# Second dense layer: plain products for the first 512 tokens, seven-product blocks of 448 for the rest

## The chip, the cores and the metric

One Trainium2 chip; the program uses one of its cores. The time of a run is the device time in microseconds (us), from one launch. Three runs of the kernel before gave 692.82, 694.65 and 697.71 us; their median is 694.65 us. TensorE is called PE, VectorE DVE, ScalarE ACT, GpSimd POOL and SyncE SP, as in the profile.

## What is computed

Three stages follow one another: a Nystrom attention over 4 batches of 576 tokens (8 heads of 64), a mixture of 8 experts with one expert for each token, and a dense layer. All of it is in float32. The dense layer, which the change touches, is this, with x the 2304 x 512 output of the experts:

```
h = x @ w_in                   # 512 -> 2048
r = np.maximum(h, 0.0)
g = s * (r * r) + b
out = g @ w_out                # 2048 -> 512
```

## The kernel before, in words

Float32 products are made on PE from operands of type fp32r: each operand is split into a high and a low part (h = cast(x), l = x - h), and `mm3` (L969) issues three matmuls, high x high, high x low and low x high, into one PSUM bank. A matmul has a 128 x 128 stationary block and up to 512 columns of the moving operand, and here the columns are tokens. All matmuls of the experts and of the dense layer have the line L972.

The work order is not written out by hand. Every operation is handed to a planner (`Plan`) with an engine, an expected duration, what it reads and writes, a priority and operations that it must follow (`after`). `Plan.run` lists all of them in time; each engine then executes its list strictly in that order, and semaphores hold an instruction until its inputs are there. Copies and casts (`copy`) go to ACT or DVE, additions and subtractions (`minus`) to DVE or POOL, as the planner chooses.

**The dense layer before.** Tokens are taken in three groups G of 768, each of two blocks of NT = 384 (`layer2`, L1163). For each of 8 units j, the hidden rows 128j to 128j+127 and 1024+128j to 1024+128j+127 are made: two row blocks, two halves of the 512 inputs, two token blocks. Such a 2 x 2 x 2 product takes seven block products instead of eight (Strassen-Winograd), so a unit has 7 x 6 = 42 matmuls in the first product (`prod`, called l3 here). The price is additions: four of the tokens, in `tokens` (tiles tq), four of the weights in each unit, in `weights` (tiles sx), and those of the products, in `take` and `plus` (tiles xx), done by ACT and DVE. Then `square` makes g from each of four results: relu on ACT (L1202), times s and itself on DVE (L1203), high part on ACT (L1206), low part on DVE (L1208). The second product (l4) has 4 output blocks dc x 2 token blocks th x 6 = 48 matmuls in a unit. For th = 0 the sum stays in four PSUM banks (`acc2`); for th = 1 there is one bank (`accr`), which DVE adds to a stored sum (L1250, tiles sums) before the next th = 1 product may start.

**What else lies in the first group.** In G = 0 the unit's weights are split by ACT, DVE and POOL from w_in (tiles w32i) into sh, so and sx (`weights`, L1107) and from w_out (w32o) into oh and ol (`outer`, L1144), and the parts are stored in DRAM by ACT's queue (sw_d, so_d). Groups 1 and 2 only load them back, by SP's queue (tiles rh, ro, rx and rp, rq). The weights arrive as 8-byte numbers, and `convert` (L1037) turns them into float32 by three DVE operations (L1042, L1049, L1051), two on ACT and one on POOL (L1054) for each of 32 pieces. These conversions start during the experts and run on into G = 0. `tokens` splits each group's seven operands into th and a low half that overwrites its source; it is called for G = 0 after the last batch's first products (`t_at`), and for G + 1 after unit 6 of G (`ahead`). Token blocks that wait are kept in DRAM (y_d).

Of the kernel before, what the change touches and what calls it, by code (L numbers as in the profile page):

```python
# [314 lines left out]
def d_dma(nbytes):  # L315
    return nbytes / RATE


TUNE = {"ahead": (6,), "t_at": lambda st: [st[B - 1]["l1half"]], "w_at": lambda st: [st[B - 1]["l1first"]], "blk": "AADD", "pre": 2, "bias": {"DVE": 0.3, "ACT": 0.0},
        "flex": {"w2l": "P", "al": "P"}, "fill": 45.0, "slack": 0.05, "duty": 0.45, "first": 12,  # L320
# [19 lines left out]
def moe_kernel(ctx, tc, qT, kT, va, vb, emb, tau, w1, w2, win, wout, s_in, b_in, outT):  # L340
# [13 lines left out]
    big = ps.tile([128, 8, 512], F32, name="big")  # L354
# [64 lines left out]
    b_row = [fixed(row_d) for _ in range(B)]  # L419
    y_d = dr.tile([2 * NG, 2, 128, 2, NT], F32, name="y_d")  # L420
    sw_d, so_d = dr.tile([8, 128, 28, 128], F32, name="sw_d"), dr.tile([8, 2, 128, 2, 512], F32, name="so_d")
# [541 lines left out]
    def low(b):  # L963

        if b.rest is None:
            b.rest = at(b, b.shape, F32R)
        return b.rest
# [105 lines left out]
    ops2 = {}  # L1073
# [4 lines left out]
    def tokens(G, first, then):  # L1078

        pr = 30000 + 1000 * G - 500  # L1080
        back = []
        for i in (2 * G, 2 * G + 1):
            if not G:
                back.append(y[i])
                continue
# [12 lines left out]
        minus(n, v(b12), v(b22), v(b12), "ta", r=[b22], w=[b12], prio=pr + 1, after=first)  # L1098
        minus(n, v(t4), v(b21), v(t2), "ta", r=[b21, t2], w=[t4], prio=pr + 1)
        ops2[G] = {}  # L1100
        for i, (p, b) in enumerate(((1, b11), (2, b21), (5, t1), (6, t2), (7, b12), (4, t4), (3, b22))):
            h = S_([128, 2, NT], F32R, nm="th")
            copy(n, v(h), v(b), "yh", r2=True, r=[b], w=[h], prio=pr + 2 + i, after=first if i < 2 else then)
            minus(n, lambda b=b: low(b), v(b), lambda h=h: h.t.bitcast(F32), "yl", r=[h], w=[b], prio=pr + 2 + i)
            ops2[G][p] = (h, b)

    def weights(G, j, pr, after):  # L1107

        a, d, js = w32i[j // 2], w32i[j // 2 + 4], 128 * (j % 2)
        q = lambda b, c, n=2: lambda: b.t[:, c:c + n, js:js + 128]  # L1110
        if G:
            sx, sh, so = (S_([128, n, 128], F32R, nm=nm) for n, nm in ((8, "rx"), (14, "rh"), (6, "ro")))
            for b, o, n in ((sh, 0, 14), (so, 14, 6), (sx, 20, 8)):
                dma(512 * 128 * n, lambda b=b, o=o, n=n: nc.sync.dma_start(b.t.bitcast(F32), sw_d[j, :, o:o + n, :]), r=[(c_sw, (j, o))], w=[b],
                    prio=pr, kind="lds", after=after)
            return choose(sx, sh, so, lambda: sx.t, 0)
# [12 lines left out]
        for b, o, n, v in ((sh, 0, 14, lambda: sh.t), (so, 14, 6, lambda: so.t), (sx, 20, 8, lambda: low(sx))):  # L1129
            store(512 * 128 * n, lambda o=o, n=n, v=v: nc.scalar.dma_start(sw_d[j, :, o:o + n, :], v().bitcast(F32)), r=[b], w=[(c_sw, (j, o))],  # L1130
                  prio=pr + 4, kind="sts")
        return choose(sx, sh, so, lambda: low(sx), 1)

    def choose(sx, sh, so, rest, parts):
# [9 lines left out]
    def outer(G, j, pr, first):  # L1144
# [16 lines left out]
        return oh, ol  # L1161

    def layer2(G):  # L1163
        mm = (NT + 32) / 2400.0
# [6 lines left out]
        def unit(j, last, early):  # L1171
            pu = pr + 10 * j
            left = weights(G, j, pu - 10, [ops2["firsts"][-2 if G else -1]] if last else TUNE["w_at"](st))
            bank = {k: Q("hp2") for k in "abc"}
# [25 lines left out]

            def square(i, src, b):
                A("ACT", d_actp(NT), lambda: nc.scalar.activation(out=rr[i].t, in_=src(), func=AF.Relu), r=[b], w=[rr[i]], prio=pu, kind="rr")  # L1202
                A("DVE", d_dve(NT), lambda: nc.vector.scalar_tensor_tensor(  # L1203
                    out=rr[i].t, in0=src(), scalar=sbc[:, 0:1], in1=rr[i].t, op0=ALU.mult, op1=ALU.mult), r=[b, (c_sb, 0)],
                  w=[rr[i]], prio=pu, kind="q")
                A("ACT", d_act(NT), lambda: nc.scalar.activation(  # L1206
                    out=gh[i].t, in_=rr[i].t, func=AF.Identity, bias=bbc[:, 0:1]), r=[rr[i], (c_sb, 1)], w=[gh[i]], prio=pu, kind="gh")
                A("DVE", d_dve(NT), lambda: nc.vector.scalar_tensor_tensor(  # L1208
                    out=low(rr[i]), in0=rr[i].t, scalar=bbc[:, 0:1], in1=gh[i].t.bitcast(F32), op0=ALU.add, op1=ALU.subtract),
                  r=[gh[i], (c_sb, 1)], w=[rr[i]], prio=pu, kind="gl")  # L1210
            first = prod(1, "a", [(b, -1) for b in rr + gh], [last] if last else [st[B - 1]["l1last"]])
# [4 lines left out]
            square(0, view(x11), x11)  # L1216
            full = prod(5, "c", after=[two_])
# [4 lines left out]
            plus(x22, "a")  # L1222
            square(3, view(x22), x22)
            prod(4, "a")
            square(2, pv("a"), bank["a"])
            prod(3, "c")
            plus(x12, "c")
            square(1, view(x12), x12)
            if G + 1 < NG and j == TUNE["ahead"][0]:
# [4 lines left out]
            for dc in range(4):  # L1234
                for th in range(2):
# [19 lines left out]
                    if j == 7:  # L1255
                        ob = sums[dc]
                        if not th:
                            ob = S_([128, NT], nm="ob")
                            copy(NT, view(ob), lambda ac=ac: ac.t[:, 0:NT], "ob", ps=True, r=[ac], w=[ob], prio=pu + 15)
                        t0 = 2 * NT * G + NT * th  # L1260
                        dma(128 * 4 * NT, lambda dc=dc, ob=ob, t0=t0: nc.sync.dma_start(
# [22 lines left out]
    def second_layer(gates):  # L1284
        convert_all(gates)
        for i in range(2, 2 * NG):
            for c, b in enumerate(y[i]):
                b.keep = False
                store(256 * 4 * NT, lambda i=i, c=c, b=b: nc.scalar.dma_start(y_d[i, c], b.t), r=[b], w=[(c_yd, (i, c))],
                      prio=4000 + 500 * i, kind="spy")  # L1290
        tokens(0, TUNE["t_at"](st), TUNE["t_at"](st))
        for G in range(NG):
            layer2(G)
# [97 lines left out]
```

## Time and profile before

| | |
|---|---|
| runs, us | 692.82, 694.65, 697.71 (median 694.65) |
| profiled execution, us | 691.78 |
| its span from the first to the last instruction, us | 689.9 |
| mean granted TensorE clock, share of 2.4 GHz | 0.979 |
| PE busy | 645.2 us (94%), 5066 matmuls |
| DVE, ACT, POOL busy | 487.7, 304.9, 229.0 us (71%, 44%, 33%) |
| DMA moved | 132.98 MB |

An engine's busy time counts the time in which it has at least one instruction; a matmul's own duration is longer than the distance to the next, since matmuls overlap. Stages are read from the times of the program's tiles: the experts end and the dense layer begins at 271.6 us, and PE's last matmul starts at 682.5 us.

### The profile page before, as it was taken

The page shows a single profiled execution, that of the slowest core. Times are in us where ns is not written, and L with a number is a line of the kernel's source. Part 1 is how long each engine was busy: PE and PEld are TensorE (multiplying, and loading weights), DVE is VectorE, ACT ScalarE, POOL GpSimd, SP SyncE. Part 2 cuts the span into 40 slices and gives each one's busy share as a digit, 9 for nine tenths or more (in the row PEclk, how much of TensorE's full clock was granted, in tenths as well). Part 3 has the DMA queues.
Part 4 walks back from the last instruction along what each step waited for, and adds up shares of the span by engine and source line. Part 5 has one row for each costly group of instructions (what it writes and reads, how often), then busy time and mean ns, then how long its engine had stood idle before and what let it go on. Part 6 is the DMA issues. An engine that isn't in the chain of part 4 may idle for free.

```text
span 689.9 us, 13153 instructions
## 1 busy us (share of the span) xinstructions
PE 645.2 (94%) x5066; PEld 601.5 (87%) x5066; DVE 487.7 (71%) x1015; ACT 304.9 (44%) x634; POOL 229.0 (33%) x197
## 2 busy tenths in 40 slices
PE   7799989999999999889879989999998999999995
PEld 5577778878998999789779878999998999999995
DVE  6976678696687789999788895645557754556551
ACT  2257345545546545555344542533335344333331
POOL 3633531523455756764356761000006200000000
PEclk9999999999999999999889999999999999999999
DMA  6619763765568382457553648844556476555102
GB/s 220 229 45 337 249 192 120 242 188 186 172 195 266 126 296 107 198 199 259 199 206 146 229 182 271 293 169 168 191 206 229 150 273 236 203 179 195 63 0 97
DMA packets 55576, 132.98 MB, mean 193 GB/s; under 512 B 5024, under 2 KB 25032, under 8 KB 55504
## 3 DMA queue, kind: packets, MB, share of 16 engines
q1 hardware_dynamic: 46208, 101.74, 43.8%
q10 hardware_dynamic: 9296, 30.30, 11.3%
q8 instruction: 42, 0.69, 0.4%
q14 instruction: 30, 0.25, 0.1%
HBM read 98.19 MB, written 33.84 MB: 191 GB/s over the span
## 4 chain that ended last, share of the span: by engine, by line
PE 72%; DVE 18%; ACT 3%; DMA 3%; issue 2%; SPq 1%; POOL 1%; DVEq 0%; ACTq 0%; POOLq 0%
PE big L972 64%; DVE rr L1208 4%; DVE rr L1203 3%; DMA vv<-in_va 2%; PE big L825 2%; PE big L945 1%; DVE xx L1198 1%; DVE y L1076 1%; PE big L644 1%; PE big L723 1%; DVE sums L1250 1%; PE big L699 1%; DMA w1s<-in_w 1%; DVE tq L1076 1%; PE big L687 1%
## 5 line engine op out<-in xcount | busy, mean ns | idle before, releaser
L1250 DVE TENSOR_TENSOR sums<-big,sums 128x384 f32<-128x384 f32 x84 | 46.6, 554 | 60.7 <-PE big L972 60.5
L972 PE MATMUL big<-gh,rp 128*128 128x384 f32 x256 | 86.4, 337 | 3.0 <-DVE sums L1250 3.0
L972 PE MATMUL big<-gh,rq 128*128 128x384 f32 x256 | 86.2, 337 | 0.0
L972 PE MATMUL big<-rr,rp 128*128 128x384 f32 x256 | 86.1, 336 | 0.0
L1208 DVE SCALAR_TENSOR_TENSOR rr<-rr,bbc,gh 128x384 fp32r<-128x384 f32 x96 | 75.2, 804 | 5.9 <-ACT gh L1206 5.9
L972 PE MATMUL big<-hh,w2h 128*128 128x288 f32 x256 | 78.3, 306 | 0.0
L1206 ACT ACTIVATE gh<-rr,bbc 128x384 fp32r<-128x384 f32 x96 | 58.5, 617 | 41.1 <-DVE rr L1203 39.8
L972 PE MATMUL big<-hl,w2h 128*128 128x288 f32 x256 | 75.7, 296 | 0.0
L1198 DVE TENSOR_TENSOR xx<-big,xx 128x384 f32<-128x384 f32 x72 | 39.7, 555 | 50.6 <-PE big L972 50.0
L972 PE MATMUL big<-hh,w2s 128*128 128x288 f32 x256 | 75.2, 294 | 0.0
L972 PE MATMUL big<-th,rh 128*128 128x384 f32 x224 | 75.0, 335 | 0.0
L508 ACT COPY xx<-big 128x384 f32<-128x384 f32 x55 | 26.0, 474 | 88.8 <-PE big L972 88.3
L1202 ACT ACTIVATE rr<-xx 128x384 f32<-128x384 f32 x72 | 37.8, 525 | 60.4 <-DVE xx L1198 60.2
L1203 DVE SCALAR_TENSOR_TENSOR rr<-xx,sbc,rr 128x384 f32<-128x384 f32 x72 | 53.3, 746 | 11.9 <-ACT rr L1202 9.5
L972 PE MATMUL big<-gh,oh 128*128 128x384 f32 x128 | 47.0, 367 | 8.9 <-DVE sums L1250 8.1
L972 PEld LDWEIGHTS big<-hh,w2h 128*128 128x128 f32 x256 | 48.0, 187 | 4.3 <-issue 3.1
L972 PEld LDWEIGHTS big<-gh,rp 128*128 128x128 f32 x256 | 48.6, 190 | 3.3 <-DVE sums L1250 3.3
L959 POOL TENSOR_TENSOR w2s<-w2s,w2h 128x1024 fp32r<-128x1024 f32 x16 | 38.3, 2413 | 32.1 <-PE big L945 18.1
L972 PEld LDWEIGHTS big<-rr,rp 128*128 128x128 f32 x256 | 48.6, 190 | 0.0
L972 PEld LDWEIGHTS big<-gh,rq 128*128 128x128 f32 x256 | 48.5, 190 | 0.0
L972 PE MATMUL big<-rr,oh 128*128 128x384 f32 x128 | 45.8, 358 | 2.7 <-DVE rr L1208 2.7
L972 PEld LDWEIGHTS big<-hl,w2h 128*128 128x128 f32 x256 | 48.1, 188 | 0.2 <-DVE hl L1000 0.2
(242 smaller groups left out, 1726.6 us busy)
## 6 DMA issues: line engine op xcount, KB each, us to landing
rh<-sw_d SPq DMA_DIRECT2D x16, 896.0 KB, 6.8
w1s<-in_w SPq DMA_DIRECT2D x16, 512.0 KB, 5.5
w2s<-in_w SPq DMA_DIRECT2D x16, 512.0 KB, 4.8
sg<-in_win SPq DMA_DIRECT2D x16, 512.0 KB, 5.1
sg<-in_wout SPq DMA_DIRECT2D x16, 512.0 KB, 3.9
rx<-sw_d SPq DMA_DIRECT2D x16, 512.0 KB, 3.9
rp<-so_d SPq DMA_DIRECT2D x16, 512.0 KB, 3.7
rq<-so_d SPq DMA_DIRECT2D x16, 512.0 KB, 4.6
```

The source lines that it names most:

```text
L508: nc.scalar.copy(out=out(), in_=in_()) if e == "ACT" else nc.vector.tensor_copy(out=out(), in_=in_())
L644: nc.tensor.matmul(xp.t[r_, 64 * g + 32 * lo:64 * g + 64], cur()[r_, g, 0, :], cur()[r_, g, lo:2, :], start=True, stop=True)
L825: nc.tensor.matmul(xp.t[:n, g, 0:264], s_[g].t[:, t0:t0 + n], m_.t[:, g, :], start=(i == 0), stop=(i == 2))
L959: two(1024, lambda e, ws=ws, wh=wh: e.tensor_tensor(out=low(ws), in0=ws.t, in1=wh.t.bitcast(F32), op=ALU.subtract), "w2l", r=[wh], w=[ws], ...
L972: nc.tensor.matmul(out, w, x, start=s, stop=e, skip_group_check=more)
L1076: return two(n, lambda e: e.tensor_tensor(out=out(), in0=a(), in1=b(), op=op), kind, **kw)
L1198: A("DVE", d_dve(NT), lambda: nc.vector.tensor_tensor(out=x.t, in0=pv(k)(), in1=x.t, op=ALU.add), r=[bank[k]], w=[x], prio=pu, kind="l6")
L1202: A("ACT", d_actp(NT), lambda: nc.scalar.activation(out=rr[i].t, in_=src(), func=AF.Relu), r=[b], w=[rr[i]], prio=pu, kind="rr")
L1203: A("DVE", d_dve(NT), lambda: nc.vector.scalar_tensor_tensor(out=rr[i].t, in0=src(), scalar=sbc[:, 0:1], in1=rr[i].t, op0=ALU.mult, op1=AL ...
L1206: A("ACT", d_act(NT), lambda: nc.scalar.activation(out=gh[i].t, in_=rr[i].t, func=AF.Identity, bias=bbc[:, 0:1]), r=[rr[i], (c_sb, 1)], w= ...
L1208: A("DVE", d_dve(NT), lambda: nc.vector.scalar_tensor_tensor(out=low(rr[i]), in0=rr[i].t, scalar=bbc[:, 0:1], in1=gh[i].t.bitcast(F32), op ...
L1250: nc.vector.tensor_tensor(out=sums[dc].t, in0=ac.t[:, 0:NT], in1=sums[dc].t, op=ALU.add)
```

## The change

The first 512 tokens become a block of their own, in which the first product is made plainly: per unit two row blocks x four pieces of the input x three = 24 matmuls of 512 columns, and 24 for the second product, with all sums kept in PSUM (`first_block`). Its weights are the plain parts ph and pl (`plain`). The other 1792 tokens are two groups of two blocks of 448 with seven products as before. Group 1 makes and stores the sums and parts of the seven products' weights, group 2 loads them; oh and ol are made and stored in the first block, and both groups load them. `ahead` goes from unit 6 to unit 3, and the first weights and tokens are released somewhat later (`w_at`, `t_at`). Buffers for ph and pl are new; lines that only rename are left out here.

```diff
-NT, NG = 384, 3
-BLOCKS = [(NT * i, NT) for i in range(2 * NG)]
+NT, NG = 448, 3
+BLOCKS = [(0, 512)] + [(512 + NT * i, NT) for i in range(4)]
...
-TUNE = {"ahead": (6,), "t_at": lambda st: [st[B - 1]["l1half"]], "w_at": lambda st: [st[B - 1]["l1first"]], "blk": "AADD", "pre": 2, "bias": {"DVE": 0.3, "ACT": 0.0},
+TUNE = {"ahead": (3,), "s_at": 2, "t_at": lambda st: [st[B - 1]["l1last"]], "w_at": lambda st: [st[B - 1]["l1half"]], "blk": "AADD", "pre": 2, "bias": {"DVE": 0.3, "ACT": 0.0},
...
+        if not G:
+            ops2[0] = []
+            for b in y[0]:
+                b.keep = False
+                h = S_([128, 2, 512], F32R, nm="th")
+                copy(1024, lambda h=h: h.t, lambda b=b: b.t, "yh", r2=True, r=[b], w=[h], prio=pr, after=first)
+                minus(1024, lambda b=b: low(b), lambda b=b: b.t, lambda h=h: h.t.bitcast(F32), "yl", r=[h], w=[b], prio=pr)
+                ops2[0].append((h, b))
+            return
...
-        if G:
+        if G == 2:
...
+    def plain(j, pr, after):
+
+        js, out = 128 * (j % 2), []
+        for a in (w32i[j // 2], w32i[j // 2 + 4]):
+            h, l = (S_([128, 4, 128], F32R, nm=nm) for nm in ("ph", "pl"))
+            src = lambda a=a: a.t[:, :, js:js + 128]
+            copy(512, lambda h=h: h.t, src, "wsh", r2=True, r=[a], w=[h], prio=pr, after=after)
+            minus(512, lambda l=l: l.t, src, lambda h=h: h.t.bitcast(F32), "wsl", r=[a, h], w=[l], prio=pr)
+            out.append((h, l))
+        return out
...
+    def first_block():
+        n = BLOCKS[0][1]
+        mm, pr = (n + 32) / 2400.0, 30000
+        acc, xs = [Q("acc2") for _ in range(4)], ops2[0]
...
+        def unit(j, last):
+            pu = pr + 10 * j
+            left = plain(j, pu - 10, last[:1] if last else TUNE["w_at"](st))
+            rr, gh = [S_([128, n], nm="rr") for _ in range(2)], [S_([128, n], F32R, nm="gh") for _ in range(2)]
+            done = []
+            for x in range(2):
+                bank, (h, l) = Q("hp2"), left[x]
+
+                def f(bank=bank, h=h, l=l):
+                    for c in range(4):
+                        xh, xl = xs[c // 2]
+                        mm3(bank.t[:, 0:n], (h.t[:, c, :], l.t[:, c, :]), (xh.t[:, c % 2, :], low(xl)[:, c % 2, :]), c == 0, c == 3)
...
+                square(n, rr[x], gh[x], lambda bank=bank: bank.t[:, 0:n], bank, pu)
...
+            if j == TUNE["ahead"][0]:
+                tokens(1, [done[0]], [done[0]])
+            oh, ol = outer(0, j, pu, done[0])
+            for dc in range(4):
+                def f(dc=dc):
+                    sl = slice(128 * dc, 128 * dc + 128)
+                    for x in range(2):
+                        mm3(acc[dc].t[:, 0:n], (oh.t[:, x, sl], ol.t[:, x, sl]), (gh[x].t, low(rr[x])), j == 0 and x == 0, j == 7 and x == 1)
+                A("PE", 6 * mm + LAP["PE"], f, r=[oh, ol, *gh, *rr], w=[acc[dc]], prio=pu + 15, kind="l4")
...
-            left = weights(G, j, pu - 10, [ops2["firsts"][-2 if G else -1]] if last else TUNE["w_at"](st))
+            left = weights(G, j, pu - 10, [ops2["firsts"][-2 if G == 2 else -TUNE["s_at"]]])
...
         tokens(0, TUNE["t_at"](st), TUNE["t_at"](st))
-        for G in range(NG):
+        first_block()
+        for G in range(1, NG):
             layer2(G)
```

The planner lists the operations anew. On DVE, in the middle of group 0, the list before has the low parts (rr, L1208) among the sums of weight parts (sx), the stored sums (L1250) and the conversions (sg, w32i, L1042 and L1051):

```order
L1208 SCALAR_TENSOR_TENSOR rr_4149<-rr_4090,bbc,gh_4107 128x384
L1076 TENSOR_TENSOR sx_4153<-sx_4095,sh_4070 128x1024
L1208 SCALAR_TENSOR_TENSOR rr_4164<-rr_4130,bbc,gh_4151 128x384
L1203 SCALAR_TENSOR_TENSOR rr_4161<-big,sbc,rr_4161 128x384
L1250 TENSOR_TENSOR sums_3917<-big,sums_3917 128x384
L1208 SCALAR_TENSOR_TENSOR rr_4186<-rr_4119,bbc,gh_4147 128x384
L1208 SCALAR_TENSOR_TENSOR rr_4194<-rr_4161,bbc,gh_4184 128x384
L1250 TENSOR_TENSOR sums_3948<-big,sums_3948 128x384
L1051 SCALAR_TENSOR_TENSOR w32i_4054<-sg_3598,w32i_4054 128x4x128
L1042 TENSOR_SCALAR sg_3795<-sg_3795 128x512
L1042 TENSOR_SCALAR sg_4068<-sg_4068 128x512
L1250 TENSOR_TENSOR sums_4031<-big,sums_4031 128x384
```

On DVE after the change, the whole of unit 3 of the first block, with the first two operations for the tokens of group 1 behind it (L1182 and L1187 are the new lines of L1203 and L1208, `big` is PSUM):

```order
L508 CAST oh_4046<-w32o_2980 128x512
L508 CAST oh_4046<-w32o_3234 128x512
L1182 SCALAR_TENSOR_TENSOR rr_4042<-big,sbc,rr_4042 128x512
L1076 TENSOR_TENSOR ol_4054<-w32o_3234,oh_4046 128x512
L1187 SCALAR_TENSOR_TENSOR rr_4070<-rr_4042,bbc,gh_4058 128x512
L1182 SCALAR_TENSOR_TENSOR rr_4072<-big,sbc,rr_4072 128x512
L1076 TENSOR_TENSOR pl_4088<-w32i_3461,ph_4056 128x512
L1187 SCALAR_TENSOR_TENSOR rr_4092<-rr_4072,bbc,gh_4086 128x512
L1076 TENSOR_TENSOR tq_4100<-y_4060,y_4044 128x896
L1076 TENSOR_TENSOR y_4110<-y_4044,th_4078 128x896
```

A unit has eight DVE operations here; the additions of products and the stored sums are not among them, and no conversion stands behind unit 2. On POOL after the change, in group 1, the sums (sx) and parts (so) of the weights, which stood in group 0:

```order
L1076 TENSOR_TENSOR sx_4679<-w32i_3050 128x256
L1076 TENSOR_TENSOR sx_4679<-w32i_2924,w32i_3050 128x256
L1076 TENSOR_TENSOR sx_4679<-sx_4679,w32i_2924 128x256
L1076 TENSOR_TENSOR sx_4679<-w32i_2924,sx_4679 128x256
L1076 TENSOR_TENSOR so_4741<-w32i_2924,sh_4708 128x512
L1076 TENSOR_TENSOR sx_4849<-w32i_3461 128x256
```

Before, POOL's list holds nothing in group 1 but seven token operations for group 2; now it holds 32 weight operations and seven token operations.

## Rows read from the trace of the kernel before

**Rows 1.** Stages by window, dense-layer matmuls alone: window, length, busy (count), clock, DMA.
```profile
271.60:418.00 146.40, 127.88 (x667) 120.86 (x665) 0.94 0.55 207
526.60:541.00 14.40, 11.39 (x56) 10.92 (x54) 0.88 0.47 170
541.00:682.70 141.70, 141.70 (x817) 141.40 (x816) 1.00 0.44 154
```

**Rows 2.** Timeline of PE: start, duration, what; two matmuls 180 apart, two 800 apart.
```profile
226.02 0.29 PE L972 MATMUL big<-hl,w2h 128*128 128x288 f32 x1
...
250.02 0.29 PE L972 MATMUL big<-hl,w2h 128*128 128x288 f32 x1
...
543.83 0.34 PE L972 MATMUL big<-th,rh 128*128 128x384 f32 x1
...
682.53 0.34 PE L972 MATMUL big<-gh,rq 128*128 128x384 f32 x1
```

**Rows 3.** Timeline of PE: the dense layer's first matmul, and a stop in group 0.
```profile
271.61 0.34 PE L972 MATMUL big<-th,sh 128*128 128x384 f32 x1
...
334.28 0.69 PE L972 MATMUL big<-gh,oh 128*128 128x384 f32 x1 [3.44 <-DVE sums L1250]
334.76 0.52 PE L972 MATMUL big<-rr,oh 128*128 128x384 f32 x1
...
339.56 0.46 PE L972 MATMUL big<-rr,oh 128*128 128x384 f32 x1
```

**Rows 4.** Waits of PE from 272 to 545 us: total, times, longest.
```profile
PE big L972 <- DVE sums L1250: 11.1, 8, 3.4
PE big L972 <- DVE xx L1198: 3.8, 4, 2.2
```

**Rows 5.** All instructions by window: length, PE, PEld, DVE, ACT, POOL busy, clock.
```profile
272.00:418.00 146.00, 127.48 (x664) 120.46 (x662) 129.27 (x177) 70.45 (x128) 88.66 (x67) 0.94 0.55 207
418.00:520.00 102.00, 102.00 (x588) 101.83 (x589) 55.06 (x100) 37.37 (x74) 0.00 (x0) 1.00 0.63 220
520.00:545.00 25.00, 22.00 (x116) 21.36 (x116) 20.92 (x25) 12.15 (x22) 14.63 (x7) 0.93 0.59 207
```

**Rows 6.** DVE's groups from 272 to 418 us: count, busy us, mean ns, idle before.
```profile
L1208 DVE SCALAR_TENSOR_TENSOR rr<-rr,bbc,gh 128x384 fp32r<-128x384 f32 x32 | 34.4, 1098 | 1.4 <-ACT gh L1206 1.4
L1203 DVE SCALAR_TENSOR_TENSOR rr<-xx,sbc,rr 128x384 f32<-128x384 f32 x24 | 23.9, 1009 | 3.0 <-ACT rr L1202 2.4
L1198 DVE TENSOR_TENSOR xx<-big,xx 128x384 f32<-128x384 f32 x24 | 13.1, 551 | 2.0 <-PE big L972 1.4
...
L508 DVE CAST oh<-w32o 128x512 fp32r<-128x512 f32 x11 | 7.5, 707 | 0.0
L1203 DVE SCALAR_TENSOR_TENSOR rr<-big,sbc,rr 128x384 f32<-128x384 f32 x8 | 4.9, 608 | 0.3 <-ACT rr L1202 0.3
...
L1051 DVE SCALAR_TENSOR_TENSOR w32o<-sg,w32o 128x512 int32<-128x512 int32 x6 | 4.8, 797 | 0.0
L1076 DVE TENSOR_TENSOR ol<-w32o,oh 128x512 fp32r<-128x512 f32 x5 | 4.3, 867 | 0.0
L1076 DVE TENSOR_TENSOR sx<-sx,sh 128x1024 fp32r<-128x1024 f32 x3 | 3.6, 1214 | 0.0
...
L1049 DVE TENSOR_SCALAR w32o<-sg 128x512 int32<-128x512 int32 x5 | 2.0, 423 | 0.1
...
L1023 DVE TENSOR_TENSOR y<-big,grow 128x288 f32<-128x288 f32 x1 | 0.5, 457 | 0.0
```

**Rows 7.** The same view from 418 to 520 us, where POOL is idle.
```profile
L1208 DVE SCALAR_TENSOR_TENSOR rr<-rr,bbc,gh 128x384 fp32r<-128x384 f32 x25 | 14.8, 611 | 1.7 <-ACT gh L1206 1.7
```

**Rows 8.** Timelines of POOL and of DVE, around 283 us.
```profile
283.02 2.71 POOL L1076 TENSOR_TENSOR sx<-sx,sh 128x1024 fp32r<-128x1024 f32 x1
...
282.38 3.77 DVE L1208 SCALAR_TENSOR_TENSOR rr<-rr,bbc,gh 128x384 fp32r<-128x384 f32 x2
```

**Rows 9.** DVE's groups from 418 to 545 us: a low half of the tokens.
```profile
L1076 DVE TENSOR_TENSOR tq<-tq,th 128x768 fp32r<-128x768 f32 x4 | 5.4, 1360 | 0.0
```

More of the change, by code (lines that the diff above doesn't have):

```diff
@@ L419, in moe_kernel @@
     b_row = [fixed(row_d) for _ in range(B)]
-    y_d = dr.tile([2 * NG, 2, 128, 2, NT], F32, name="y_d")
+    y_d = dr.tile([len(BLOCKS), 2, 128, 2, NT], F32, name="y_d")
     sw_d, so_d = dr.tile([8, 128, 28, 128], F32, name="sw_d"), dr.tile([8, 2, 128, 2, 512], F32, name="so_d")
@@ L1080, in tokens @@
         pr = 30000 + 1000 * G - 500
+        if not G:
[7 more added lines that the diff above has]
+            return
         back = []
[L1082 to L1085, printed above, removed]
+        for i in (2 * G - 1, 2 * G):
             back.append([S_([128, 2, NT], nm="y") for _ in range(2)])
@@ L1161, in outer, with square @@
         return oh, ol
+    def square(n, rr, gh, src, b, pu):
+        A("ACT", d_actp(n), lambda: nc.scalar.activation(out=rr.t, in_=src(), func=AF.Relu), r=[b], w=[rr], prio=pu, kind="rr")
+        A("DVE", d_dve(n), lambda: nc.vector.scalar_tensor_tensor(
+            out=rr.t, in0=src(), scalar=sbc[:, 0:1], in1=rr.t, op0=ALU.mult, op1=ALU.mult), r=[b, (c_sb, 0)],
+          w=[rr], prio=pu, kind="q")
+        A("ACT", d_act(n), lambda: nc.scalar.activation(
+            out=gh.t, in_=rr.t, func=AF.Identity, bias=bbc[:, 0:1]), r=[rr, (c_sb, 1)], w=[gh], prio=pu, kind="gh")
+        A("DVE", d_dve(n), lambda: nc.vector.scalar_tensor_tensor(
+            out=low(rr), in0=rr.t, scalar=bbc[:, 0:1], in1=gh.t.bitcast(F32), op0=ALU.add, op1=ALU.subtract),
+          r=[gh, (c_sb, 1)], w=[rr], prio=pu, kind="gl")
@@ new lines, in first_block @@
+    def first_block():
[13 more added lines that the diff above has]
+                        mm3(bank.t[:, 0:n], (h.t[:, c, :], l.t[:, c, :]), (xh.t[:, c % 2, :], low(xl)[:, c % 2, :]), c == 0, c == 3)
+                done.append(A("PE", 12 * mm + LAP["PE"], f, r=[h, l, *(b for x_ in xs for b in x_)], w=[bank, (rr[x], -1), (gh[x], -1)],
+                              prio=pu, kind="l3", after=last or [st[B - 1]["l1last"]]))
+                square(n, rr[x], gh[x], lambda bank=bank: bank.t[:, 0:n], bank, pu)
+            ops2.setdefault("firsts", []).append(done[0])
+            if j == TUNE["ahead"][0]:
[7 more added lines that the diff above has]
+                A("PE", 6 * mm + LAP["PE"], f, r=[oh, ol, *gh, *rr], w=[acc[dc]], prio=pu + 15, kind="l4")
+                if j == 7:
+                    ob = S_([128, n], nm="ob")
+                    copy(n, lambda ob=ob: ob.t, lambda dc=dc: acc[dc].t[:, 0:n], "ob", ps=True, r=[acc[dc]], w=[ob], prio=pu + 15)
+                    dma(512 * n, lambda dc=dc, ob=ob: nc.sync.dma_start(outT[128 * dc:128 * dc + 128, 0:n], ob.t), r=[ob], prio=pu + 95,
+                        kind="out")
+            return done
+        last = None
+        for j in range(8):
+            last = unit(j, last)
+        ops2["mark"] = last[1]
@@ L1199, in plus @@
                   r=[bank[k]], w=[x], prio=pu, kind="l6")
[L1201 to L1211, printed above, removed]
+            first = prod(1, "a", [(b, -1) for b in rr + gh], [last])
             ops2.setdefault("firsts", []).append(first)
@@ L1215, in unit @@
             plus(x11, "b")
-            square(0, view(x11), x11)
+            square(NT, rr[0], gh[0], view(x11), x11, pu)
             full = prod(5, "c", after=[two_])
@@ L1222, in unit @@
             plus(x22, "a")
-            square(3, view(x22), x22)
+            square(NT, rr[3], gh[3], view(x22), x22, pu)
             prod(4, "a")
-            square(2, pv("a"), bank["a"])
+            square(NT, rr[2], gh[2], pv("a"), bank["a"], pu)
             prod(3, "c")
             plus(x12, "c")
-            square(1, view(x12), x12)
+            square(NT, rr[1], gh[1], view(x12), x12, pu)
             if G + 1 < NG and j == TUNE["ahead"][0]:
@@ L1259, in unit @@
                             copy(NT, view(ob), lambda ac=ac: ac.t[:, 0:NT], "ob", ps=True, r=[ac], w=[ob], prio=pu + 15)
-                        t0 = 2 * NT * G + NT * th
+                        t0 = BLOCKS[2 * G - 1 + th][0]
                         dma(128 * 4 * NT, lambda dc=dc, ob=ob, t0=t0: nc.sync.dma_start(
@@ L1285, in second_layer @@
         convert_all(gates)
-        for i in range(2, 2 * NG):
+        for i in range(1, len(BLOCKS)):
             for c, b in enumerate(y[i]):
@@ L1289, in second_layer @@
                 store(256 * 4 * NT, lambda i=i, c=c, b=b: nc.scalar.dma_start(y_d[i, c], b.t), r=[b], w=[(c_yd, (i, c))],
-                      prio=4000 + 500 * i, kind="spy")
+                      prio=4500 + 700 * i, kind="spy")
         tokens(0, TUNE["t_at"](st), TUNE["t_at"](st))
-        for G in range(NG):
+        first_block()
+        for G in range(1, NG):
             layer2(G)
```

2 rows, old and new, of the table plan are left out of this document.

## The prediction

> **What bounds the kernel now.** I read the stages first, then PE's own pace, then who makes PE wait, and last what fills the engine it waits for.
>
> PE is 94% busy, but that is a mean over stages that differ. From 541 to 682.7 us it never stops; from 526.6 to 541 us it is busy for 11.4 of 14.4 us, and from 271.6 to 418 us for 127.9 of 146.4 us, with a granted clock of 0.94 [rows 1]. Its undisturbed pace comes from two pairs of matmuls. With 288 columns 180 of them take 250.02 - 226.02 = 24.00 us, 133.3 ns each; with 384 columns 800 take 138.70 us, 173.4 ns each [rows 2]. That is 96 columns in 40.1 ns, one column in 0.417 ns, and 13.4 ns a matmul that do not depend on the columns.
>
> So the dense layer's 2160 matmuls of 384 columns need 2160 x 0.1734 = 374.5 us of PE. They take 411.1 us, from 271.61 [rows 3] to the end of the last one at about 682.7 [rows 2]. 36.6 us are lost. By the counts of the windows, 146.4 - 667 x 0.1734 = 30.8 us go in the first stretch and 14.4 - 56 x 0.1734 = 4.7 in the second [rows 1]; a window also counts matmuls cut by its edges, so I take 31.6 and 5. The third loses nothing.
>
> Within them PE waits for DVE: for the stored sums 11.1 us, for the additions of products 3.8 [rows 4]. The wait is only a part of the price. After the stop of 3.44 us at 334.28 the matmuls start 4.80 us / 15 = 0.32 us apart until 339.56 [rows 3], at the lower clock of 1.2 GHz, instead of 0.173.
>
> DVE is late because it has too much to do in group 0: 129.3 us busy out of 146, 88.5%, where the group's 720 matmuls need 124.8 us of PE; POOL has 88.7 us beside it. From 418 to 520 us, where POOL is idle, DVE is busy for 55 of 102 us and PE loses nothing [rows 5]. Part of DVE's load is not its own: the low part (L1208) takes 0.611 us with POOL idle [rows 7] and 1.098 in group 0 [rows 6]. At 282.38 two of them take 3.77 us, against 1.22 when undisturbed, while one POOL operation lasts 2.71 [rows 8]. So this stage is bound by the side work of DVE and POOL, the two later groups by PE.
>
> **The change part by part.** *PE's own work.* By the pace above, a matmul takes 200.1 ns with 448 columns and 226.7 with 512. The two groups have 2 x 720 of the first, 288.1 us; the first block has 8 x 48 = 384 of the second, 87.1. The sum is 375.2 us instead of 374.5: **+0.6 us** (the unrounded difference). The plain block does an eighth more in the first product, but 336 matmuls fewer save their 13.4 ns each.
>
> The Trainium skill, page "TensorE: Matmul & The Clock Gate", section "Wait — 56ns, not 53.3ns?", gives columns / 2.4 GHz plus about 2.5 ns for warm matmuls. With that fixed part the layers would be 351.0 and 355.3 us, and the change would cost 4.3 us on PE. The fp32r matmuls of this case show 13.4 ns [rows 2], and the measurement decides.
>
> *The first block instead of group 0.* Gone from it are the additions of products (24 on DVE at 0.551 us [rows 6], 13.2 us, and 24 copies), the stored sums, and all sums of weight parts. Eight units need 87.1 us of PE. DVE's list for this stretch, priced with group 0's means [rows 6], so with POOL's disturbance in them: between 288 and 384 columns a simple operation grows from 0.457 to 0.551 us, about 1 ns a column, and I add 0.125 us for 128 columns.
> - 16 squares from PSUM at 0.608 + 0.125: 11.7 us;
> - 16 low parts at 1.098 + 0.125: 19.6;
> - 16 splits of weights (ol, pl) at 0.867: 13.9;
> - 11 casts of 512 columns at 0.707 and one of 1024 at 1.2: 9.0;
> - conversions: 5 at 0.797, 4 at 0.423 and 4 priced as casts: 8.5 (before, 26 DVE conversions were left after the experts, now 13: 13 go to the experts' stretch, where seven-product tokens and one weight set left DVE);
> - seven token operations of 896 columns for group 1 at 1.360 [rows 9] + 0.125: 10.4;
> - weights of group 1's first two units: two of 1024 at 1.214 and five of at most 0.867: 6.8.
>
> Together 79.9 us. If DVE again reaches only 88.5% of a stretch, these need 90.3 us, **3.2 us more than PE**. The lower bound: with the low parts undisturbed (0.611 + 0.125) the sum is 72.1 us, 81.5 us of stretch, and nothing is lost. The upper bound: the loss rate of group 0, 31.6 / 124.8 = 25%, which gives 22 us. I take 3.2, since the sum rests on the same rows as the stage it replaces. It also has better cover: PE's order is first product of unit j + 1, second product of j, so that a unit's squares have the second product of j - 1 and the first of j + 1 to hide behind, 48 x 0.2267 = 10.9 us.
>
> *Group 1 gets the weight work.* The sums and splits for seven products, DRAM stores included, lie in group 1 now. DVE there, again at group 0's means (plus 0.06 for 64 columns): 32 low parts 37.2, 24 squares from SBUF 25.7, 8 from PSUM 5.4, 24 additions and 28 stored sums at 0.614 31.9, 3 copies 1.8, weights 4 x 1.214 + 6 x 0.867 + 1.2 = 11.3, 4 token operations 5.9: 119.2 us, against 144.0 of PE. Divided by 0.885 it is 134.7, still below 144.0. With low parts and squares undisturbed it is 94. POOL's 39 operations need at most about its load in group 0 (88.7 us) and fit. So on average the work is hidden by PE; the cost if that cover is gone is a quarter of 144, 36 us. What is not average is the preparation of the next group's tokens: 18 operations between the units' own, which cost the 5 us at 526.6 before. It comes again, in unit 3 instead of 6, with weight work beside it: **5 us**, between 0 and 12.
>
> *DMA and queues.* ACT's queue stores 1792 KB a unit in group 1 where SP's queue loaded 1792 KB; the volume in that stage is the same, and there the DMA share was 0.63 with PE full [rows 5]. The token loads of group 1 stand on SP behind the last conversion's load and ahead of the rp loads, as before. Released by unit 3, about 30 us into the block, they have some 55 us before group 1. I cost this at nothing. The experts before 271.6 us and the 7 us after the last matmul have the same matmuls and outputs; nothing.
>
> *Sum.* 691.8 (profiled execution) - 36.6 + 0.6 + 3.2 + 5 = **664.0 us**. The median of the runs shown is 694.65, 0.41% above the profiled 691.78; in these terms the forecast is **667 us**. Its own range is 660 to 680.
>
> **Rivals.**
> - *Nothing is lost any more*: the tokens prepared at unit 3 find gaps, the first block keeps its cover. 691.8 - 36.6 + 0.6 = 655.8, as a median 658.5. For it: groups 1 and 2 ran without loss wherever DVE stood at 54% [rows 5]. Against: the first block's DVE stands at 92% of PE's time.
> - *The first block jams as group 0 did*, 22 us instead of 3.2, because conversions, tokens and the first weights of group 1 come in bursts: 682.8, median 685.6. For it: 92%, and rows 8. Against: the 10.9 us of cover in each unit.
> - *Group 1 inherits the jam*, since the weight work moved there rather than away: 36 us in place of 5 gives 695.0, median 697.9, no measurable change. For it: POOL's blocking moves along. Against: 119 of 144 us.
> - *Slower: the half clock through the first block.* Its matmuls come in groups of 24, 5.4 us each; if PE waits about 2 to 3 us ahead of each, as at 334.28, every group starts at 1.2 GHz and at worst all 384 run at 0.32 x 512/384 = 0.427 us, 164 us instead of 87.1. With the 5 us, 691.8 - 36.6 + 0.6 + 76.9 + 5 = 737.7, median 740.8. It decides from where a unit's side work is more than about 2.3 us longer than the 10.9 of PE, that is 105 us of DVE for the block. For it: one wait was enough for 5 us of low clock. Against: 79.9 is far from 105.
>
> **How the numbers follow.** The forecast gets 0.67, no loss 0.12, the jam in the first block 0.10, in group 1 0.07, the half clock 0.04. About 1% can be told from no change, so faster ends at 687.7. The first three are faster: 0.89; the fourth is the same: 0.07; the last is slower: 0.04. The range reaches down to 657, just under the no-loss case, and up to 686, over the jam in the first block; some 0.1 lies above it and little below.
>
> **What would show it.** Right: PE's matmuls at 200 and 227 ns; the dense layer's first matmul near 271.6 us; PE nearly full from there to some 359 us and waiting mainly around tokens; DVE near 90% busy in that stretch and about 80% in group 1; stored sums no longer the first of PE's waits early in the layer. Wrong: waits of 2 us and more ahead of each group of 24 with PEclk under 0.9; a dense layer that starts late because the experts lost DVE to the earlier conversions; or the losses of group 0 found again in group 1 with PE waiting for L1309.

## The result, and the profile after

Four runs of the kernel after gave 671.57 to 677.69 us, median 672.61; four of the kernel before on the same chip 691.81 to 697.71, median 693.74. The ratio is 0.970, with a 95% interval of 0.964 to 0.977: 3% faster, 5.6 us above the forecast of 667 and inside its range of 660 to 680. The profiled execution took 671.57 us, its span is 669.8 us and its mean granted clock 0.988.

The stages, all instructions, first the first block, then groups 1 and 2. The columns are those of [rows 5]: window, length, PE, PEld, DVE, ACT and POOL busy, clock, DMA.

```profile
270.50:359.60 89.10, 87.95 (x387) 71.68 (x386) 77.52 (x90) 45.58 (x74) 48.43 (x31) 1.00 0.50 187
359.60:514.70 155.10, 148.37 (x722) 134.45 (x721) 102.36 (x133) 67.86 (x118) 54.30 (x39) 1.00 0.49 182
514.70:661.60 146.90, 146.18 (x721) 134.93 (x719) 72.46 (x117) 53.32 (x95) 0.00 (x0) 1.00 0.38 140
```

In the first block DVE is as full as it was in group 0, 77.5 of 89.1 us or 87% (88.5% in [rows 5]), and yet PE is busy for all but 1.15 us, at a granted clock of 1.00. The forecast had this from the cover in a plain unit; the runs on releases and widths below bear on that. Group 1 leaves PE idle for 6.7 us.

What PE waits for from 270 to 662 us, to be held against [rows 4] (total, times, longest):

```profile
PE big L972 <- DVE xx L508: 2.3, 2, 1.7
PE big L972 <- DVE xx L1267: 1.8, 2, 1.0
PE big L972 <- DVE sums L1309: 1.7, 2, 1.0
PE big L972 <- ACT xx L508: 1.3, 1, 1.3
PE big L972 <- DVE rr L1182: 1.3, 2, 0.9
```

The stored sums, 11.1 us before, are down to 1.7, one of them 0.7 us at the end of the layer. DVE's groups in the first block, from 270 to 360 us, which answer to [rows 6]:

```profile
L1187 DVE SCALAR_TENSOR_TENSOR rr<-rr,bbc,gh 128x512 fp32r<-128x512 f32 x16 | 21.4, 1338 | 3.0 <-ACT gh L1185 3.0
L1182 DVE SCALAR_TENSOR_TENSOR rr<-big,sbc,rr 128x512 f32<-128x512 f32 x16 | 11.9, 747 | 5.8 <-ACT rr L1181 5.8
L1076 DVE TENSOR_TENSOR pl<-w32i,ph 128x512 fp32r<-128x512 f32 x8 | 6.9, 866 | 0.0
L1076 DVE TENSOR_TENSOR ol<-w32o,oh 128x512 fp32r<-128x512 f32 x8 | 6.6, 823 | 0.3 <-ACT oh L508 0.3
```

The low part (L1187) still takes 1.338 us here, beside POOL; with 448 columns it takes 0.790 us in group 1 and 0.679 in group 2, where POOL is idle.

The timeline of PE: the layer's first matmul, two in group 2 that are 640 apart, the only stop of group 2, and the last matmul.

```profile
270.51 0.40 PE L972 MATMUL big<-th,ph 128*128 128x512 f32 x1
...
520.15 0.37 PE L972 MATMUL big<-th,rh 128*128 128x448 f32 x1
...
649.85 0.37 PE L972 MATMUL big<-rr,rp 128*128 128x448 f32 x1
...
660.26 0.47 PE L972 MATMUL big<-gh,rp 128*128 128x448 f32 x1 [0.72 <-DVE sums L1309]
...
661.39 0.37 PE L972 MATMUL big<-gh,rq 128*128 128x448 f32 x1
```

129.70 us / 640 = 202.7 ns with 448 columns, not the 200.1 of the forecast. With 512 columns 229 steps of the first block from 288 to 340 us give 226.6 ns, as forecast.

By these paces each stage's loss is the time from its first matmul to the next stage's, less the number of matmuls times the pace. The first block took 89.07 us, 384 x 0.2267 = 87.05: **2.0 us lost**. Group 1 took 155.10 us, 720 x 0.2027 = 145.94: **9.2 us**. Group 2 lost **1.0 us**. For the kernel before the same reckoning with 173.4 ns gives 31.5, 5.1 and 0. So the lost time falls from 36.6 to 12.2 us, while PE's own work grows from 374.5 to 378.9: the change wins back lost time and saves no work of PE. The experiments are read in these terms: first block (or group 0), group 1, group 2.

One stop of group 1 shows how it comes about; timelines of DVE, POOL and PE:

```profile
470.69 2.81 DVE L1182 SCALAR_TENSOR_TENSOR rr<-xx,sbc,rr 128x448 f32<-128x448 f32 x1
473.61 0.62 DVE L508 COPY xx<-big 128x448 f32<-128x448 f32 x1
...
470.26 2.77 POOL L1076 TENSOR_TENSOR sx<-sx,sh 128x1024 fp32r<-128x1024 f32 x1 [1.65 <-DVE sh L508]
...
474.29 0.47 PE L972 MATMUL big<-th,sh 128*128 128x448 f32 x1 [1.71 <-DVE xx L508]
```

The square takes 2.81 us instead of the 0.68 it needs in group 2: it ends at 473.50, just after POOL's low part of the weight sums at 473.03, and the copy that PE waits for stands behind it. The Trainium skill, page "SBUF — State Buffer", section "SBUF: two separate sides", has a lock on a shared port pair for this: a GpSimd instruction, or a VectorE one with two inputs from SBUF, holds the pair for its whole length and the other blocks. The 2.81 us agree with it; no run here takes the lock alone.

### The profile page after: what moved, and what is told of

Read it like the earlier page. It is cut to its first block, busy times and chain, and to the rows that moved or that the text cites. A ratio compares the mean times of both kernels' runs of the same rounds, so it can differ in the third digit from the quotient of the medians.

```text
span 669.8 us, 12285 instructions
## 1 busy us (share of the span) xinstructions
PE 638.7 (95%) x4730; PEld 561.0 (84%) x4730; DVE 461.5 (69%) x928; ACT 301.5 (45%) x600; POOL 225.0 (34%) x192
## 4 chain that ended last, share of the span: by engine, by line
PE 79%; DVE 13%; ACT 3%; issue 2%; DMA 1%; SPq 1%; POOL 0%; DVEq 0%; ACTq 0%; POOLq 0%
PE big L972 70%; PE big L825 2%; DVE rr L1182 2%; PE big L945 1%; DVE rr L1187 1%; DMA vv<-in_va 1%; PE big L644 1%; PE big L723 1%; PE big L699 1%; PE big L687 1%; DVE sg L1042 1%; DVE xx L1267 1%; SPq L536 1%; DVE y L1023 0%; PE big L663 0%
## 5 line engine op out<-in xcount | busy, mean ns | idle before, releaser
L972 PE MATMUL big<-gh,rp 128*128 128x448 f32 x256 | 94.0, 367 | 2.4 <-DVE sums L1309 1.7
L972 PE MATMUL big<-gh,rq 128*128 128x448 f32 x256 | 93.6, 365 | 0.0
L972 PE MATMUL big<-rr,rp 128*128 128x448 f32 x256 | 93.4, 365 | 0.0
L1187 DVE SCALAR_TENSOR_TENSOR rr<-rr,bbc,gh 128x448 fp32r<-128x448 f32 (+1 forms) x80 | 67.7, 856 | 12.9 <-ACT gh L1185 12.6
L1309 DVE TENSOR_TENSOR sums<-big,sums 128x448 f32<-128x448 f32 x56 | 34.8, 622 | 52.5 <-PE big L972 52.4
L1185 ACT ACTIVATE gh<-rr,bbc 128x448 fp32r<-128x448 f32 (+1 forms) x80 | 53.9, 679 | 30.2 <-DVE rr L1182 29.9
L508 ACT COPY xx<-big 128x448 f32<-128x448 f32 x44 | 23.2, 527 | 69.8 <-PE big L972 69.8
L1182 DVE SCALAR_TENSOR_TENSOR rr<-xx,sbc,rr 128x448 f32<-128x448 f32 x48 | 42.9, 896 | 8.7 <-ACT rr L1181 8.4
L972 PEld LDWEIGHTS big<-hh,w2s 128*128 128x128 f32 x256 | 48.2, 188 | 0.0
L972 PE MATMUL big<-th,sh 128*128 128x448 f32 x112 | 41.5, 371 | 5.0 <-DVE xx L508 2.3
L972 PE MATMUL big<-ah,v1h 128*128 128x288 f32 x128 | 40.9, 320 | 2.4 <-DVE y L1023 2.4
```

Source lines behind the costliest of these rows:

```text
L508: nc.scalar.copy(out=out(), in_=in_()) if e == "ACT" else nc.vector.tensor_copy(out=out(), in_=in_())
L972: nc.tensor.matmul(out, w, x, start=s, stop=e, skip_group_check=more)
L1182: A("DVE", d_dve(n), lambda: nc.vector.scalar_tensor_tensor(out=rr.t, in0=src(), scalar=sbc[:, 0:1], in1=rr.t, op0=ALU.mult, op1=ALU.mult) ...
L1185: A("ACT", d_act(n), lambda: nc.scalar.activation(out=gh.t, in_=rr.t, func=AF.Identity, bias=bbc[:, 0:1]), r=[rr, (c_sb, 1)], w=[gh], prio ...
L1187: A("DVE", d_dve(n), lambda: nc.vector.scalar_tensor_tensor(out=low(rr), in0=rr.t, scalar=bbc[:, 0:1], in1=gh.t.bitcast(F32), op0=ALU.add, ...
L1309: nc.vector.tensor_tensor(out=sums[dc].t, in0=ac.t[:, 0:NT], in1=sums[dc].t, op=ALU.add)
```

## The experiments

### The weight work of group 0, left out of the kernel before

```diff
+        if j:
+            sx, sh, so = ops2["one"]
+            ...
+            return choose(sx, sh, so, lambda: low(sx), 1)
         sx = S_([128, 8, 128], nm="sx")
...
+        ops2["one"] = sx, sh, so
```

> The kernel before; in group 0 all eight units use the split weights and sums of unit 0 (tiles sx, sh, so), so seven eighths of the work that makes them on ACT, DVE and POOL is left out; the stores, the matmuls, the additions of products and the stored sums stay. Theory 1 (group 0 is bound by the side work of DVE and POOL): its loss on PE falls from 31.6 us to under 12 and the time to 667-675 us. Rival (the seven products' own chain of additions and stored sums makes PE wait): the loss stays above 20 us and the time above 682 us.

Measured: 672.09 us, ratio 0.969 (0.962 to 0.975). The losses are 11.2, 4.9 and 0 us. From 272 to 418 us:

```profile
272.00:418.00 146.00, 138.87 (x779) 134.29 (x778) 108.66 (x179) 67.23 (x130) 43.17 (x28) 1.00 0.65 241
```

POOL has 43 us of work instead of 88.7, DVE 109 instead of 129, and 779 matmuls run where 664 did [rows 5]; the low part falls from 1.098 to 0.734 us. The seven products' own chain was all still there, so theory 1 holds: 20 of the 31.5 us that group 0 loses come from this part of the side work. The 11.2 us that are left were not taken apart; the conversions, the casts of w_out and that chain are all still in them.

### Group 1 after the change: weights, tokens, both

The first run has the edit above in the kernel after; the second this one; the third both.

```diff
+        if G == 2:
+            ops2[2] = ops2[1]
+            return
         back = []
```

> The kernel after; in group 1 all eight units use the split weights and sums of unit 0, so seven eighths of the weight work of that group is left out; stores and matmuls stay. Theory 1 (what group 1 loses on PE, 9 us above its pace, comes from the weight work that moved there): the loss falls to 2-3 us and the time by 6-7 us, to about 665 us. Rival (the loss comes from the tokens of group 2 that are prepared in that group): the loss stays at 7 us or more, and the time within 2 us of the kernel after.

> The kernel after; group 2 uses the token operands of group 1 again, so the four loads and the 18 operations that prepare its own are left out. Theory 1 (weight work makes group 1's loss of 9 us): the loss stays at 6 us or more, the time within 3 us of the kernel after. Rival (the tokens make it, as the forecast had it with 5 us): the loss falls to 2-4 us and the time by 5-7 us.

> The kernel after; group 1 uses unit 0's weight parts in all units, and group 2 uses group 1's tokens: both of the runs that left out one of them, together. Theory 1 (group 1's loss of 9 us above a pace of 202.7 ns has two sources that share DVE and POOL, so that each alone took away only 2 to 3 us of it): the loss falls to 1-3 us, as in group 2. Rival (the seven products' own additions and stored sums make it): the loss stays at 5 us or more.

Measured, with the losses in order:

| left out | us (ratio, interval) | first block, group 1, group 2 |
|---|---|---|
| weights | 675.75 (0.972; 0.966 to 0.978) | 4.6, 7.7, 3.8 |
| tokens | 672.48 (0.968; 0.962 to 0.974) | 2.1, 7.1, 3.8 |
| both | 667.60 (0.965; 0.962 to 0.969) | 6.3, 1.7, 3.8 |

Each of the first two runs refutes one cause. Without the weights the loss does not fall to the 2 to 3 us of its theory 1, and without the tokens it does not fall to the 2 to 4 us of its rival; it stays above 7 us in both, so neither kind of work makes the loss of group 1 alone. (The time without the weights is 3 us above the kernel after, since the first block and group 2 lose more.) Of the 7.7 and 7.1 us, 0.9 and 1.3 are a slower pace of the matmuls (last section). Stops, with the slow matmuls behind them, make 9.1 us of the loss after the change, 6.7 without the weights, 5.8 without the tokens and 0.2 without both, as theory 1 of the third run had it.

Two stops, in the timelines of DVE, POOL and PE, the first without the weights, the second without the tokens:

```profile
443.06 3.02 DVE L1076 TENSOR_TENSOR tq<-tq,th 128x896 fp32r<-128x896 f32 x1
...
447.86 0.74 PE L972 MATMUL big<-gh,rp 128*128 128x448 f32 x1 [2.68 <-DVE sums L1316]
...
461.75 2.34 POOL L1076 TENSOR_TENSOR so<-w32i,sh 128x512 fp32r<-128x512 f32 x2 [0.70 <-ACT sh L508]
...
462.05 1.46 DVE L1190 SCALAR_TENSOR_TENSOR rr<-rr,bbc,gh 128x448 fp32r<-128x448 f32 x1
...
464.10 0.48 PE L972 MATMUL big<-gh,rp 128*128 128x448 f32 x1 [1.77 <-DVE sums L1312]
```

Without the weights PE stops for 2.7 us up to 447.86. A low half of the tokens on DVE stands ahead of squares and a stored sum; it takes 3.02 us (of four of this size in the first block after the change three take 1.09 us on average and one takes 3.00). Without the tokens PE stops for 1.8 us up to 464.10: a low part on DVE takes 1.46 us beside weight parts on POOL, ahead of a stored sum. Each kind of work shares DVE and POOL with the units' own operations, and either is enough to make these late. With both left out PE does not stop once in group 1. The windows of groups 1 and 2 with both left out are alike:

```profile
366.00:513.60 147.60, 147.60 (x721) 135.03 (x720) 72.02 (x116) 53.92 (x96) 0.00 (x0) 1.00 0.45 170
513.60:663.20 149.60, 148.88 (x721) 134.89 (x720) 72.60 (x117) 53.56 (x95) 0.00 (x0) 1.00 0.38 137
```

What stands under group 1 there (1.7 us), and most of group 2's 3.8, is no stop but another pace (last section). The first block of the two runs without the weights lost more (4.6 and 6.3 us), with a stop of 1.7 and 1.8 us up to some 359 us. The planner makes all lists anew for every edit, so a stage can change by a few us although the edit was aimed at another one; a single difference of that size in these tables can't be read as an effect.

### The releases alone, and the change without them

In the kernel before, the new line with `ahead`, `t_at` and `w_at`; in the kernel after, the old one.

```diff
-"ahead": (6,), "t_at": ... "l1half" ..., "w_at": ... "l1first"
+"ahead": (3,), "t_at": ... "l1last" ..., "w_at": ... "l1half"
```

> The kernel before with the changed times of release alone (tokens of the next group from unit 3, first tokens and weights later). Theory 1 (the gain is the plain first block's, and the jam of group 0 is untouched by releases): 688-697 us, the loss of 31.6 us in group 0 stays within 5 us; at most the 5 us at the change from group 1 to group 2 go. Rival (the times of release bring a good part of the gain): 683 us or less.

> The kernel after with the times of release of the kernel before (tokens of the next group from unit 6, first tokens and weights earlier). Theory 1 (the releases matter little beside the plain first block, as the forecast had them): 668-677 us, within 1% of the kernel after. Rival (the releases were made for this order, as their cost of 7 us in the order before lets one think): 678 us or more.

Measured: the old blocks with the new releases 701.84 us, ratio 1.011 (1.005 to 1.017), the new blocks with the old releases 693.58, ratio 1.002 (0.999 to 1.005). Theory 1 fell in both; the rival fell in the first run and held in the second. With the kernel before at 692 to 694 and the kernel after at 672.6, **neither half of the change brings anything alone** (the releases in the old blocks make it 1% slower); together they bring 21 us.

In the old blocks with the new releases group 0 loses 39.6 us instead of 31.5. PE waits 1.8 us for its first tokens up to 277.73, and the longest stop stands behind a cast of weight sums (DVE and PE):

```profile
403.21 1.03 DVE L508 CAST sh<-sx 128x1024 fp32r<-128x1024 f32 x1
...
404.30 0.69 PE L972 MATMUL big<-th,sh 128*128 128x384 f32 x1 [8.83 <-DVE sh L508]
```

The layer starts at 274.59 us there instead of 271.61, but that is not shown to be an effect: with the first releases as in the kernel after, the layer starts anywhere from 270.1 to 275.7 us. In the new blocks with the old releases the losses are 8.3, 21.1 and 1.0 us. PE's waits there, from 272 to 535 us:

```profile
PE big L972 <- DVE sums L1309: 7.7, 5, 5.8
PE big L972 <- DVE rr L1182: 5.1, 3, 2.6
PE big L972 <- DVE sx L1076: 4.4, 1, 4.4
```

### Which release it is

> The kernel after with the next group's tokens prepared from unit 6 instead of unit 3, the first tokens and weights released as in it. With all three old times of release the profiled execution loses 6.3 us more in the first block, 12 us more in group 1, and its dense layer starts 1.9 us later. Theory 1 (the tokens' place makes the loss in group 1, and part of that in the first block, where group 1's tokens would be made last): 684-692 us, of it a stop of 5 us or more in unit 7 of group 1. Rival (the early first weights and tokens make it): 671-676 us.

> The kernel after with the first tokens and weights released as early as in the kernel before, the next group's tokens from unit 3. Theory 1 (the tokens' place counts): 672-678 us, at most the 1.9 us later start and some 3 us in the first two units more than the kernel after. Rival (the early release fills DVE before the layer starts and the order never recovers): 684 us or more.

> The kernel after with the next group's tokens from unit 4. Theory 1 (the later they are released, the fewer units are left to spread 18 operations over): between the kernel after and the run with unit 6, 673-682 us. Rival (any unit with two or more left is enough): within 3 us of the kernel after.

> The kernel after with the next group's tokens from unit 2. Theory 1 (an earlier release spreads the operations more): 668-673 us, group 1 losing 6-9 us instead of 9. Rival (in unit 2 of the first block they meet the last conversions, DVE's heaviest stretch there): 675 us or more, with the loss in the first block.

| tokens from unit, first weights and tokens | us (ratio, interval) | first block, group 1, group 2 |
|---|---|---|
| 3, late (the change) | 672.61 (0.970; 0.964 to 0.977) | 2.0, 9.2, 1.0 |
| 3, early | 676.81 (0.977; 0.972 to 0.982) | 9.6, 6.2, 1.0 |
| 6, late | 685.93 (0.992; 0.988 to 0.995) | 3.2, 21.8, 1.0 |
| 6, early | 693.58 (1.002; 0.999 to 1.005) | 8.3, 21.1, 1.0 |
| 4, late | 671.53 (0.970; 0.966 to 0.975) | 3.7, 6.6, 3.8 |
| 2, late | 676.84 (0.977; 0.972 to 0.983) | 2.1, 11.8, 3.7 |

Theory 1 held in time for unit 6 and for the early first release; for unit 4 it fell, and its rival held. The tokens' place decides: unit 6 costs 13.3 us, nearly all in group 1. It comes in several stops, the longest of 4.39 us in group 1's first unit, not in one of 5 us or more in unit 7 as theory 1 had it. Two stops of that run, in the timelines of DVE and PE:

```profile
364.96 1.62 DVE L1076 TENSOR_TENSOR y<-y,th 128x896 fp32r<-128x896 f32 x1
366.50 1.14 DVE L1187 SCALAR_TENSOR_TENSOR rr<-rr,bbc,gh 128x448 fp32r<-128x448 f32 x1
367.56 1.21 DVE L1076 TENSOR_TENSOR sx<-sx,sh 128x1024 fp32r<-128x1024 f32 x1
...
487.61 2.53 DVE L508 CAST th<-y 128x896 fp32r<-128x896 f32 x1
...
368.83 0.74 PE L972 MATMUL big<-th,sx 128*128 128x448 f32 x1 [4.39 <-DVE sx L1076]
...
492.51 0.65 PE L972 MATMUL big<-gh,rp 128*128 128x448 f32 x1 [3.69 <-DVE sums L1309]
```

Tokens that are made last in the first block are still on DVE when group 1 begins, ahead of the weight part that its first unit needs; and those of group 2 come into its last units, ahead of a stored sum. The early first release costs the first block instead, which loses 7.6 us more, with stops of 2.6 and 3.2 us before squares in its first two units; group 1 loses 3.0 us less. Unit 4 can't be told from unit 3 (its profile is of an execution of 678.82 us whose layer began at 275.7), and unit 2 is worse: theory 1 fell there, but not as its rival had it, since the loss is in group 1 (11.8 us).

### The width of the plain block

```diff
-NT, NG = 448, 3
-BLOCKS = [(0, 512)] + [(512 + NT * i, NT) for i in range(4)]
+NT, NG = 512, 3
+BLOCKS = [(0, 256)] + [(256 + NT * i, NT) for i in range(4)]
...
```

The other run has 464 and 448 in these places. Both also give the first block's operands this size (left out here).

> The kernel after with a first block of 256 tokens and groups of 2 x 512. Theory 1 (the plain block wins by its width, since its PE time covers DVE's side work): the first block needs 46 us of PE but some 63 us of DVE, takes 70 us or more, or passes the work on to group 1, and the time is 685-695 us, near the kernel before. Rival (PE's own sum decides, 372.5 us against 379.0): 665-668 us. 512 columns run at 226.7 ns here too.

> The kernel after with a first block of 448 tokens and groups of 2 x 464. Pace: if only 448 columns are off the line through 288, 384 and 512 columns, 464 columns take 207 ns (and the first block's 448 columns 203-207); if the pace above 384 columns has steps of its own, 464 takes 210 ns or more. Time, theory 1 (the first block's DVE work hardly shrinks, 74 us of it stand against 78 us of PE, and PE loses 7 us there instead of 2): 670-677 us. Rival (PE's own sum decides): 2-3 us less than the kernel after.

Measured with 256: 698.27 us, ratio 1.011 (1.006 to 1.015). The first block, and its longest stop in the timeline of PE:

```profile
271.20:355.90 84.70, 55.36 (x386) 52.83 (x385) 77.05 (x92) 37.75 (x73) 52.66 (x33) 0.84 0.50 185
...
339.15 0.58 PE L972 MATMUL big<-th,ph 128*128 128x256 f32 x1 [17.45 <-ACT ph L508]
```

DVE is busy for 77 us, as with 512 tokens, and not for the 63 us of theory 1: its squares and low parts take 23.2 us instead of 33.3, but other operations take longer. PE needs 46 us and waits, and the granted clock falls to 0.84. The stop of 17.5 us is for a cast (ph) whose conversion stood on POOL behind token and weight operations. With half the tokens the block takes 84.7 us instead of 89.1, so its length follows the side work and not its matmuls. That is the first block as a jam; 512 tokens set 87 us of PE against this work. Theory 1 held in kind, with a time some 3 us above its band.

Measured with 448: 671.09 us, ratio 0.971 (0.967 to 0.975), in theory 1's band and not to be told from the kernel after. But the 7 us that theory 1 had for the first block did not come: at its own pace of 206.7 ns it loses some 2.6 us, one stop of 2.4. The rival fell too: 464 columns take 210.0 ns, so that PE's own sum is 381.8 us, 2.9 more than in the kernel after. Of the runs that leave nothing out, this one and the one with the tokens from unit 4 come lowest, and neither can be told from the kernel after: no better version was found.

## Why the prediction came out right, and where it was wrong

On the profiled execution the sum was 664.0 us, and 671.57 came out, 7.6 more. The terms:

| term | forecast | measured | difference |
|---|---|---|---|
| pace with 448 columns, 1440 matmuls | 200.1 ns | 202.7 ns | +3.8 us |
| loss of group 1 | 5 us | 9.2 us | +4.2 us |
| loss of group 2, and the stretch from its last matmul's start to the span's end | 0 and 7.4 us | 1.0 and 8.4 us | +2.0 us |
| loss of the first block | 3.2 us | 2.0 us | -1.2 us |
| start of the layer | 271.6 us | 270.5 us | -1.1 us |

**What bounds the kernel** was right in the main: most of the jam of group 0 is side work. Leaving out seven eighths of its weight work brings as much as the whole change (0.969 against 0.970).

**The first block's term** was right in its parts. DVE was forecast with 79.9 us at 88.5% and had 77.5 at 87%; squares took 0.747 us (0.733 forecast), low parts 1.338 (1.223). That its loss of 3.2 us came close to the measured 2.0 is in part luck. The rule behind it, DVE's work divided by 0.885, gives 75.9 us for the same block with the old releases, where DVE has 67.2 us. That is less than PE's 87.1 and means no loss, but the block took 95.4 us and lost 8.3. The cover of 10.9 us in each unit is supported by the 256 tokens, which halve it and jam, but that run changes the groups' width too.

**PE's own work** was mis-sized: the line through 288 and 384 columns holds at 512, but not at 448 and 464. Its rows make +0.7 us, not +0.6; measured it is +4.4.

**Group 1's term** of 5 us was given to tokens alone. The runs show 9.2 us that belong to tokens and weights together, and to neither alone. DVE's list there was forecast too long (119.2 us against 102.4, or 66% of the stage instead of some 80%), and yet the loss was larger, so the mean load said nothing of it; what counts is which operation stands ahead of the one PE waits for.

**The step that failed** is that the releases have no term. The forecast says of the 5 us at the old change of groups "It comes again, in unit 3 instead of 6", which prices the earlier tokens at nothing, and `t_at` and `w_at` appear only as operations in the list. In the new blocks they are worth 21 us: 13.3 by unit 3 instead of 6, 4.2 by the later first release, the remaining 3.5 only by both together (4.2 and 3.5 are of the size that new lists alone can make). The rival "group 1 inherits the jam" (697.9 us, 0.07) is close in time to what the new blocks do with the old releases: 693.58, with 21.1 us lost in group 1 where the rival had 36. It was dismissed by 119 of 144 us of DVE, and that argument did not carry it: DVE had 105 of 167 us in that run. The forecast came out because the change brought the releases that kept this rival away, not because the blocks did so by themselves. That was luck: nothing in its sum tells the one order from the other.

**The other rivals.** "Nothing is lost" has its mechanism in group 1 without weights and tokens, which does not stop at all. The jam in the first block did not come (2.0 us against 22), nor did the half clock through it (granted clock 1.00); with 256 tokens, where DVE has more to do than PE, the clock fell to 0.84. The 2.3 us from which that rival was to decide are not borne out: after a stop of 2.24 us in the kernel before (411.06 us) the matmuls soon start 0.32 us apart, after one of 2.57 us with the early first release (279.48 us) they do not slow down.

## What to carry to other kernels

Price the stage by the engine that holds the side work: here a stage with little side chain and much matmul time hid what a seven-product stage could not, and with half its width it no longer did. Where a change moves work and also its times of release, give the releases a term of their own, by asking at each end of a stage what stands on the busy engine ahead of the instruction that the next stage needs first; here neither half was worth anything without the other. A mean load says that the work fits, not that it is in time: DVE was busy for 66% of group 1 where 9.2 us were lost, and for 63% where 21.1 were.

## What the runs showed of the hardware

PE's pace was taken for a straight line in the columns. At a granted clock of 1.00, 40 matmuls of 256 columns take 119.8 ns each, 288 and 384 columns 133.3 and 173.4 [rows 2], 512 columns 226.6: all on the line (120.1 at 256). 448 columns should take 200.1 and 464 206.7. 464 take 210.0 (544 steps from 546 us on) and in stretches of group 1 as little as 208.3; 448 run at one of two paces, 202.7 or 206.7 ns, each constant over a hundred matmuls and more of both products. The second, in group 2 of the run without tokens, 628 matmuls apart:

```profile
520.06 0.37 PE L972 MATMUL big<-th,rx 128*128 128x448 f32 x1
...
649.85 0.37 PE L972 MATMUL big<-gh,rp 128*128 128x448 f32 x1
```

129.79 us / 628 = 206.7 ns. In that run the pace was 202.7 until 441 us and changed at a stop of PE; in the run with early first weights it went from 206.7 back to 202.7, again at a stop. But no stop is needed: with both left out, 80 matmuls from 420.34 us take 202.7 ns each and 154 from 438.19 us 206.7, and no two between 420 and 470 us start more than 207 ns apart. 720 matmuls at the slower one cost 2.9 us, which is most of the 3.8 us of group 2 in the tables. The Trainium skill, page "TensorE: Matmul & The Clock Gate", section "Wait — 56ns, not 53.3ns?", has a fixed part of about 2.5 ns a matmul; these rows show 13.3 ns at 512 columns and 16 or 20 at 448. What sets the two paces was not tried and stays open.
